# Spreading the conversion of layer 2's last five weight units over two steps each

## The chip, the cores and the metric

One core of a Trainium2 chip runs the whole program. The metric is the device time of one execution in microseconds (us), lower is better; the median of three runs stands below. The profile is of one execution of the same kernel.

## The reference, cut to what matters

```python
# 1: linear attention with decay, over 4 x 8 heads, 768 positions, head size 48
state = alpha[t][:, None] * state + outer(k[t], v[t]);  y[t] = q[t] @ state
# 2: x is the 3072 x 384 result. Tokens with x @ w_skip > 0 go through their best one of
#    8 experts (384 -> 1024 -> 384, relu), scaled by its softmax weight, and are added to x
# 3: layer 2, on all 3072 tokens
h = x @ w_in            # w_in  384 x 2048
g = h - tanh(h)
out = g @ w_out         # w_out 2048 x 384
```

The two matrices of layer 2 arrive in 64-bit floating point (they were scaled by a 64-bit number), all other inputs in 32-bit. The kernel reads the 64-bit words as pairs of 32-bit integers and converts them itself.

## The kernel before, in words

TensorE works on rounded 32-bit values (the type fp32r of the trace). To keep the precision, each operand is split in a high part (rounded) and a low part (the remainder), and each product is three matmuls: high by high, low by high, high by low.

**Stages.** Attention runs in 24 steps, with the routing of tokens to experts between them. The first units of layer 2 for its first 512 tokens follow, then the experts: a loop of `NMU + 4` = 68 steps, one for each 128 columns of an expert's hidden layer and four to drain. Then layer 2: its 2048 hidden columns are 16 weight units of 128 (`NF2`), its tokens six blocks of 512 (`nb`). The first block's units 0 to 4 (`NE0`) were done ahead of the experts, so layer 2's loop (`steps`, lines 871 to 897) has 91 steps: units 5 to 15 of block 0 are steps 0 to 10, block 1 begins at step 11.

**One step of layer 2.** `mm1b` (line 453) issues nine matmuls of 128x512 into a PSUM bank, line 464. Its `after` is a generator with four operations: tanh on ACT (L470), `g` = h minus tanh on DVE (L472), its high part `gh` on ACT (L474), its low part `gl` on DVE (L476). Then `mm2b` of the step two before issues twelve matmuls of 128x384 (L498). The banks of `mm1b` alternate between two, so the matmuls of step i wait for `g` of step i-2, which reads that bank last. The `g` line thus stands in the trace as what TensorE waits for.

**The weight units.** Units 0 to 4 were converted during attention and units 5 to 10 during the experts. The five late ones (`NLATE`), units 11 to 15, are converted in layer 2's own first ten steps; unit 11+k is first used by step 6+k. Each is loaded by one DMA of 768 KB into `raw64`, for which there is one buffer (`wload`, line 125), and converted by four functions (`wsplit`, lines 150 to 170), which the trace shows by line:

- `s0`: DVE `cs` (L155) and DVE `ca` (L156), both reading `raw64`; they repack the upper word.
- `s1`: ACT `cl` (L159), which reads the lower words of `raw64`, DVE `cs` again (L160, called cs2 here), ACT `wh` (L162), the high part, made from `ca`.
- `s2`: DVE `cl` times `cs` (L166, called cl2 here), DVE `ca` minus `wh` (L167, called ca2 here).
- `s3`: DVE `wl` (L170), the low part.

`cs`, `ca` and `cl` have one buffer each too.

**What sets the order.** Each engine works through its own queue in the order in which the program issues to it (`tc.manual_schedule()`); the lists `at[i]` and `aft[i]` say what is issued at the start and the end of step i. A transfer waits on SP's queue until its buffer's last reader is done. In the kernel before, late unit k has its load, `s0` and `s1` at the start of step 2k and `s2` and `s3` at the start of step 2k+1, all ahead of that step's matmuls, tanh, `g`, `gh` and `gl`. At the end of steps 3, 5, 7 and 9 `split2` transposes a quarter of the next block: three transposes on TensorE (L437), the high part `xh` on ACT (L439), the low part `xl` on DVE (L440). In the experts' loop, `result` of the last unit (L587, `xe`, two DVE operations that read the last expert's sums) is issued at step `NMU + 2`.

Of the kernel before, what the change touches and what calls it, by code (L numbers as in the profile page):

```python
# [33 lines left out]
NF, NF2 = FF // 128, FF2 // 128  # L34
# [3 lines left out]
NMU = NE * NF  # L38
# [5 lines left out]
NLATE = 5  # L44
# [17 lines left out]
def tile_kernel(ctx: ExitStack, tc: tile.TileContext, att0, att, vt, wsg, wmoe, wff, out):  # L62
# [56 lines left out]
    def wload(i):  # L119
        if i < NMU or not wide:  # L120
            raw_t[i] = rings["raw"].tile([128, W], F32, tag="raw", name=f"raw{i}")
            nc.sync.dma_start(raw_t[i], wmoe[i] if i < NMU else wff[i - NMU])
        else:
            raw_t[i] = cvp.tile([128, W, 2], U32, tag="raw64", name=f"raw{i}")
            nc.sync.dma_start(raw_t[i].rearrange("p a b -> p (a b)"), wff[i - NMU].bitcast(U32))

    def wsplit(i):

        own = (ring if i % RING < RING0 else rings["ring2"]) if i < NMU else ffE if i < NMU + NE0 else None
        late = i >= NMU + NF2 - NLATE  # L130
        t_ = {}

        def alloc():
            src = own or rings["late" if late else "R"]
            t_["h"] = src.tile([128, W], F32R, tag="wh", name=f"wh{i}")
            t_["l"] = src.tile([128, W], F32R, tag="wl", name=f"wl{i}")
            w_t[i] = (t_["h"], t_["l"])

        def n0():
            alloc()  # L140
            A.copy(t_["h"], raw_t[i])  # L141

        def n1():
            V.tensor_tensor(t_["l"], raw_t[i], t_["h"].bitcast(F32), ALU.subtract)  # L144

        if i < NMU or not wide:
            return [n0, n1]


        def s0():  # L150
            up = raw_t[i][:, :, 1]
            t_["s"] = cvp.tile([128, W], U32, tag="cs", name=f"cs{i}")
            t_["a"] = cvp.tile([128, W], U32, tag="ca", name=f"ca{i}")
            t_["f"] = cvp.tile([128, W], F32, tag="cl", name=f"cl{i}")
            V.tensor_scalar(t_["s"], up, 3, 0x3FFFFFFF, ALU.logical_shift_left, ALU.bitwise_and)  # L155
            V.scalar_tensor_tensor(t_["a"], up, 0xC0000000, t_["s"], ALU.bitwise_and, ALU.bitwise_or)  # L156

        def s1():
            A.activation(t_["f"], raw_t[i][:, :, 0], AF.Copy, scale=2.0 ** -52)  # L159
            V.tensor_scalar(t_["s"], t_["a"], 0xFF800000, None, ALU.bitwise_and)  # L160
            alloc()
            A.copy(t_["h"], t_["a"].bitcast(F32))  # L162

        def s2():
            a_ = t_["a"].bitcast(F32)
            V.tensor_tensor(t_["f"], t_["f"], t_["s"].bitcast(F32), ALU.mult)  # L166
            V.tensor_tensor(a_, a_, t_["h"].bitcast(F32), ALU.subtract)  # L167

        def s3():
            V.tensor_tensor(t_["l"], t_["a"].bitcast(F32), t_["f"], ALU.add)  # L170

        return [s0, s1, s2, s3]
# [252 lines left out]
    def rload(nb):  # L425
        d = X2[nb]
        d["r"] = rowp.tile([128, 4, RW], F32, tag="rows", name=f"rows{nb}")
        r0 = NS + 512 * nb
        i_ = nc.sync.dma_start(d["r"], xb[r0:r0 + 512, :].rearrange("(a p) d -> p a d", a=4))
        if 0 < nb < NIN // 512:  # L430
            tc.declare_no_dep(i_.ins, group="expert", reason="rows that no expert writes")
# [105 lines left out]
    def xload(e):  # L537
        E[e]["xe"] = rings["xe"].tile([128, 2, RW], F32, tag="xe", name=f"xe{e}")
        i_ = nc.sync.dma_start(E[e]["xe"], xb[e * CAP:(e + 1) * CAP, :].rearrange("(a p) d -> p a d", a=2))
        if e >= 2:  # L540
            tc.declare_no_dep(i_.ins, group="expert", reason="rows that no expert writes")
# [9 lines left out]
    def mm1(i):  # L551
        e, f = divmod(i, NF)
        d = E[e]
        wh, wl = w_t[i]
        hp = psY(f"hp{i}")[:, :CAP]
        n = 0
        for k in range(KT):
            ks = slice(128 * k, 128 * k + 128)
            for w_, x_ in ((wh, d["eh"]), (wl, d["eh"]), (wh, d["el"])):
                T.matmul(hp, w_[:, ks], x_[:, k], start=n == 0, stop=n == 3 * KT - 1)  # L560
                n += 1
        hh = rings["m2"].tile([128, CAP], F32R, tag="hh", name=f"hh{i}", bufs=3)
        hl = rings["m2"].tile([128, CAP], F32R, tag="hl", name=f"hl{i}", bufs=3)
        A.activation(hh, hp, AF.Relu)
        V.scalar_tensor_tensor(hl, hp, 0.0, hh.bitcast(F32), ALU.max, ALU.subtract)  # L565
        d[f] = (hh, hl)

    def mm2(i):
        e, f = divmod(i, NF)
        d = E[e]  # L570
        wh, wl = w_t.pop(i)
        hh, hl = d.pop(f)
        if f == 0:
            d["yp"] = [psB(f"yp{e}_{a}")[:, :DM] for a in range(2)]
        for a in range(2):
            o = d["yp"][a]
            sl_ = slice(128 * a, 128 * a + 128)
            T.matmul(o, hh[:, sl_], wh[:, DM:], start=f == 0, stop=False)  # L578
            T.matmul(o, hh[:, sl_], wl[:, DM:], start=False, stop=False)  # L579
            T.matmul(o, hl[:, sl_], wh[:, DM:], start=False, stop=f == NF - 1)  # L580
        if f < NF - 1:
            return
        xe = d["xe"]

        def result():
            for a in range(2):
                V.scalar_tensor_tensor(xe[:, a, :DM], d["yp"][a], xe[:, a, CGW:CGW + 1], xe[:, a, :DM],  # L587
                                       ALU.mult, ALU.add)

        def store():  # L590
            for a in range(2):
                s_ = nc.gpsimd.indirect_dma_start(
                    xb[:, :], bass.IndirectOffsetOnAxis(xe[:, a, CPOS:CPOS + 1].bitcast(U32), 0), xe[:, a, :], None,
                    bounds_check=TOP, oob_is_err=False)
                if e or a:
                    tc.declare_no_dep(s_.ins, group="expert", reason="rows of their own")
                tc.add_to_no_dep_group("expert", s_.ins)

        at[i + 3].append(result)
        at[i + 4].append(store)  # L600
# [81 lines left out]
    at, aft = collections.defaultdict(list), collections.defaultdict(list)  # L682
# [149 lines left out]
    at, aft = collections.defaultdict(list), collections.defaultdict(list)  # L832
# [18 lines left out]
    for e in range(1, NE):  # L851
        for a in range(2):
            aft[NF * e - 4 + a].append(lambda e=e, a=a: xprep(e, a))
        if e + 1 < NE:
            at[NF * e - 1].append(lambda e=e: xload(e + 1))
    at[20].append(lambda: rload(1))
    for i in range(NMU + 4):
        for f_ in at[i]:
            f_()
        if i < NMU:  # L860
            mm1(i)
        if 2 <= i < NMU + 2:
            mm2(i - 2)
        for f_ in aft[i]:
            f_()
# [3 lines left out]
    rings["x2", 1] = pool("p1", 1, ff_ctx, "right")  # L869
    rings["g"] = pool("g1", 2, ff_ctx, "right")  # L870
    steps = [(nb, f) for nb in range(NU // 4) for f in range(NF2) if nb or f >= NE0]
    at, aft = collections.defaultdict(list), collections.defaultdict(list)
    for k in range(NLATE):
        r = NMU + NF2 - NLATE + k
        at[max(0, 2 * k - 1 + 1)].append(lambda r=r: wload(r))
        for n, f_ in zip((0, 0, 1, 1), wsplit(r)):
            at[2 * k + n].append(f_)
    for nb in range(1, NU // 4):
        i = steps.index((nb, 0))
        for a in range(4):  # L880
# [4 lines left out]
    for i in range(len(steps) + 1):  # L885
        for f_ in at[i]:
            f_()
        if i < len(steps):
            issue, after = mm1b(*steps[i])
            issue()  # L890
            collections.deque(after(), 0)
        if 2 <= i < len(steps):
            mm2b(*steps[i - 2])
        elif i == len(steps):
            mm2b(steps[-1][0], *(f for _, f in steps[-2:]))
        for f_ in aft[i]:
            f_()
# [6 lines left out]
    with tc.If(past > 0):  # L904
# [17 lines left out]
        with tc.For_i(0, NC_, 1) as ci:  # L922
            with tc.For_i(0, B, 1) as bi:
# [23 lines left out]
                for f in range(NF2):  # L947
                    wh, wl = w_t[NMU + f]
                    hpd = psY(f"hp2d{f}")[:, :128]
                    n = 0  # L950
# [75 lines left out]
```

## Time and profile before

| what | value |
|---|---|
| time, median of 3 runs (lowest to highest) | 739.13 us (737.74 to 741.64) |
| the profiled execution: time, span | 738.44 us, 736.8 us |
| granted TensorE clock, mean | 0.986 |
| busy: PE, PE's weight load, DVE, ACT, POOL | 93%, 85%, 61%, 41%, 17% |
| L472 `g`, L476 `gl` (DVE, 96 each) | 66.3 us, 66.5 us |
| L470 tanh, L474 `gh` (ACT, 96 each) | 57.3 us, 59.5 us |
| L498 matmuls, three groups of 384 | 130.2, 130.4 and 129.9 us |
| L464 matmuls, three groups of 288 | 116.2, 114.2 and 114.3 us |

A busy share is a mean over the span; matmuls are pipelined, so one that is listed as 393 ns long lets the next start after about 230 ns. Layer 2's loop begins at 323.94 us of the span and the late units are converted until 372.5 us.

### The profile page before, as it was taken

How to read it: one execution, taken by the hardware profiler on the slowest of the kernel's cores; microseconds unless marked ns; L12 is line 12 of the kernel's file. 1: busy time of each engine (PE TensorE's matmuls, PEld its weight loads, DVE VectorE, ACT ScalarE, POOL GpSimd, SP SyncE). 2: the span in 40 equal slices, each digit the busy share in tenths (PEclk: the TensorE clock that was granted, in tenths of full speed). 3: DMA queues.
4: the chain of work that ended last, by engine and by line, in shares of the span. 5: the costliest groups of instructions: out<-in, count | busy, mean ns of one | idle time of the engine just before them, and what ended most of it. 6: DMA issues, size and time to landing. Idle time of an engine off the chain costs nothing.

```text
span 736.8 us, 11897 instructions
## 1 busy us (share of the span) xinstructions
PE 686.1 (93%) x4707; PEld 629.2 (85%) x4707; DVE 449.8 (61%) x736; ACT 301.7 (41%) x588; POOL 125.3 (17%) x121
## 2 busy tenths in 40 slices
PE   3999978899999999999979999999999999999993
PEld 2888867788999999997768999999899999889892
DVE  8999999966888888847744334333333333333331
ACT  2546544345666656624422233233323333333220
POOL 5433347441011111210002001000200020001002
PEclk9999999899999999999989999999999999999997
DMA  9899957346779778512111001001100110001001
GB/s 275 180 218 281 230 145 219 98 155 207 253 257 321 257 249 268 168 64 85 45 44 43 1 1 61 25 1 44 43 1 1 45 43 1 1 1 43 2 1 46
DMA packets 30542, 81.39 MB, mean 110 GB/s; under 512 B 4405, under 2 KB 14677, under 8 KB 30480
## 3 DMA queue, kind: packets, MB, share of 16 engines
q1 hardware_dynamic: 26384, 68.64, 32.3%
q0 software_dynamic: 4096, 11.92, 4.4%
q8 instruction: 39, 0.64, 0.4%
q14 instruction: 23, 0.19, 0.1%
HBM read 65.45 MB, written 15.84 MB: 110 GB/s over the span
## 4 chain that ended last, share of the span: by engine, by line
issue 55%; PE 26%; DVE 12%; POOL 3%; ACT 1%; DMA 1%; POOLq 0%; ACTq 0%; SPq 0%; DVEq 0%
PE hp L560 8%; PE yp L578 3%; PE yp L579 3%; PE yp L580 3%; DVE G L203 2%; POOL out_dram L512 2%; DVE F L196 2%; PE pa L229 2%; DVE am L234 2%; PE py L243 2%; PE px L296 1%; PE h L464 1%; PE py L250 1%; DVE kh L214 1%; POOL qh L209 1%
## 5 line engine op out<-in xcount | busy, mean ns | idle before, releaser
L472 DVE TENSOR_TENSOR g<-h,g 128x512 f32<-128x512 f32 x96 | 66.3, 691 | 162.8 <-ACT g L470 162.8
L498 PE MATMUL y<-wh,gh 128*128 128x384 f32 x384 | 130.2, 339 | 0.7 <-ACT gh L474 0.7
L498 PE MATMUL y<-wh,gl 128*128 128x384 f32 x384 | 130.4, 340 | 0.2
L498 PE MATMUL y<-wl,gh 128*128 128x384 f32 x384 | 129.9, 338 | 0.0
L470 ACT ACTIVATE g<-h 128x512 f32<-128x512 f32 x96 | 57.3, 598 | 168.1 <-PE h L464 168.1
L464 PE MATMUL h<-xh,wh 128*128 128x512 f32 x288 | 116.2, 403 | 3.2 <-DVE g L472 3.1
L464 PE MATMUL h<-xh,wl 128*128 128x512 f32 x288 | 114.2, 397 | 3.6 <-DVE wl L170 3.6
L464 PE MATMUL h<-xl,wh 128*128 128x512 f32 x288 | 114.3, 397 | 0.0
L476 DVE TENSOR_TENSOR gl<-g,gh 128x512 fp32r<-128x512 f32 x96 | 66.5, 693 | 65.9 <-ACT gh L474 44.0
L474 ACT CAST gh<-g 128x512 fp32r<-128x512 f32 x96 | 59.5, 620 | 91.4 <-DVE g L472 91.4
L512 POOL DMA_INDIRECT out_dram<-ob,id x24 | 23.6, 983 | 375.8 <-DVE ob L511 308.0
L498 PEld LDWEIGHTS y<-wh,gh 128*128 128x128 f32 x384 | 72.4, 189 | 5.2 <-ACT gh L474 1.3
L498 PEld LDWEIGHTS y<-wl,gh 128*128 128x128 f32 x384 | 72.5, 189 | 4.2
L498 PEld LDWEIGHTS y<-wh,gl 128*128 128x128 f32 x384 | 72.3, 188 | 1.6 <-DVE gl L476 1.6
L464 PEld LDWEIGHTS h<-xh,wh 128*128 128x128 f32 x288 | 54.4, 189 | 14.5 <-DVE g L472 5.8
L464 PEld LDWEIGHTS h<-xh,wl 128*128 128x128 f32 x288 | 54.6, 190 | 12.5 <-DVE wl L170 3.9
L464 PEld LDWEIGHTS h<-xl,wh 128*128 128x128 f32 x288 | 54.5, 189 | 12.5
L141 ACT CAST wh<-raw 128x768 fp32r<-128x768 f32 x64 | 53.5, 835 | 24.1 <-PE yp L580 22.3
L144 DVE TENSOR_TENSOR wl<-raw,wh 128x768 fp32r<-128x768 f32 x64 | 60.8, 950 | 2.8 <-ACT wh L141 2.8
L560 PE MATMUL hp<-eh,wh 128*128 128x256 f32 x192 | 55.7, 290 | 1.3 <-DVE hl L565 1.3
L229 PE MATMUL pa<-qh,kh 64*128 64x128 f32 x384 | 30.8, 303 | 27.9 <-POOL qh L209 19.5
L560 PE MATMUL hp<-eh,wl 128*128 128x256 f32 x192 | 53.8, 280 | 0.0
(140 smaller groups left out, 1164.5 us busy)
## 6 DMA issues: line engine op xcount, KB each, us to landing
raw<-in_wmoe_dram SPq DMA_DIRECT2D x64, 384.0 KB, 4.0
raw<-in_wff_dram SPq DMA_DIRECT2D x16, 768.0 KB, 5.3
it<-in_att_dram SPq DMA_DIRECT2D x40, 289.5 KB, 7.9
rows<-xb SPq DMA_DIRECT2D x6, 776.0 KB, 4.3
vt<-in_vt_dram SPq DMA_DIRECT2D x24, 192.0 KB, 5.6
xb<-zero SPq DMA_DIRECT2D x4, 776.0 KB, 7.3
xe<-xb SPq DMA_DIRECT2D x8, 388.0 KB, 4.9
it<-in_att_dram SPq DMA_DIRECT2D x2, 772.0 KB, 8.5
```

The lines of the kernel that those rows point to most:

```text
L141: A.copy(t_["h"], raw_t[i])
L144: V.tensor_tensor(t_["l"], raw_t[i], t_["h"].bitcast(F32), ALU.subtract)
L229: T.matmul(d["pa"][:, j, p], d["kh"][r, p], d["qh"][r, p], start=p == 0, stop=p == NP - 1)
L464: T.matmul(hp, *todo.pop(0), start=len(todo) == last, stop=not todo)
L470: A.activation(g, hp, AF.Tanh)
L472: V.tensor_tensor(g, hp, g, ALU.subtract)
L474: A.copy(gh, g)
L476: V.tensor_tensor(gl, g, gh.bitcast(F32), ALU.subtract)
L498: T.matmul(o, g_[:, sl_], w_[:, DM:], start=first and n == 0, stop=last and n == len(todo) - 1)
L512: s_ = nc.gpsimd.indirect_dma_start(out[:, :], bass.IndirectOffsetOnAxis(d["id"][:, a:a + 1], 0), ob, None, bounds_check=N - 1, oob_is_err ...
L560: T.matmul(hp, w_[:, ks], x_[:, k], start=n == 0, stop=n == 3 * KT - 1)
L578: T.matmul(o, hh[:, sl_], wh[:, DM:], start=f == 0, stop=False)
```

## The change: what it does

The four functions of each late unit move. A third list, `mid[i]`, holds what is issued inside step i's `after`, behind `gh` and ahead of `gl`.

- Late unit 0: its load is issued at step `NMU + 1` of the experts' loop and its `s0` at step `NMU + 3`; `s1` and `s2` at the start of layer 2's step 0, `s3` in the middle of step 0.
- Late unit k from 1 to 4: its load is issued at the start of step 0, 1, 3 or 5 (before: 2, 4, 6, 8), `s0` at the start of step 2k-1, `s1` in the middle of step 2k-1, `s2` at the start of step 2k, `s3` in the middle of step 2k.

No operation is added or left out, and no buffer is changed.

```diff
+    late = [wsplit(NMU + NF2 - NLATE + k) for k in range(NLATE)]
+    at[NMU + 1].append(lambda: wload(NMU + NF2 - NLATE))
+    at[NMU + 3].append(late[0][0])
     for i in range(NMU + 4):
...
-    at, aft = collections.defaultdict(list), collections.defaultdict(list)
+    at, mid, aft = (collections.defaultdict(list) for _ in range(3))
+
     for k in range(NLATE):
-        r = NMU + NF2 - NLATE + k
-        at[max(0, 2 * k - 1 + 1)].append(lambda r=r: wload(r))
-        for n, f_ in zip((0, 0, 1, 1), wsplit(r)):
-            at[2 * k + n].append(f_)
+        if k:
+            at[max(0, 2 * k - 3)].append(lambda k=k: wload(NMU + NF2 - NLATE + k))
+            at[2 * k - 1].append(late[k][0])
+        (mid[2 * k - 1] if k else at[0]).append(late[k][1])
+        at[2 * k].append(late[k][2])
+        mid[2 * k].append(late[k][3])
...
             issue, after = mm1b(*steps[i])
             issue()
-            collections.deque(after(), 0)
+            for n, _ in enumerate(after()):
+                if n == 2:
+                    for f_ in mid[i]:
+                        f_()
```

## Rows read from the trace of the kernel before

**Rows 1.** Stretches: busy us (instructions) of PE, PEld, DVE, ACT, POOL; PEclk, DMA, GB/s.

```profile
323.94:378.88 54.94, 48.16 (x220) 40.48 (x220) 40.67 (x59) 21.32 (x35) 2.25 (x2) 0.94 0.24 78
600.00:700.00 100.00, 100.00 (x508) 90.50 (x507) 36.03 (x55) 31.34 (x53) 3.89 (x4) 1.00 0.02 9
```

**Rows 2.** Timeline of PE, steps 0 to 12: start, us, line, [idle before, releaser].

```profile
323.94 0.40 PE L464 MATMUL h<-xh,wh 128*128 128x512 f32 x1
...
328.44 0.50 PE L464 MATMUL h<-xh,wh 128*128 128x512 f32 x1 [0.21 <-DVE g L472]
...
368.47 0.51 PE L464 MATMUL h<-xh,wh 128*128 128x512 f32 x1 [0.60 <-DVE g L472]
372.58 0.79 PE L464 MATMUL h<-xh,wl 128*128 128x512 f32 x1 [3.60 <-DVE wl L170]
...
378.88 0.39 PE L464 MATMUL h<-xh,wh 128*128 128x512 f32 x1
...
383.09 0.39 PE L464 MATMUL h<-xh,wh 128*128 128x512 f32 x1
```

**Rows 3.** Timeline of PE, transposes of a later block, with nothing to wait for.

```profile
416.61 0.49 PE L437 MATMUL px<-ident,rows 128*128 128x128 f32 x3
...
417.17 0.39 PE L464 MATMUL h<-xh,wl 128*128 128x512 f32 x1
```

**Rows 4.** Waits, 320 to 380 us: who for whom, us, times, longest.

```profile
PE h L464 <- DVE g L472: 3.1, 8, 0.7
```

**Rows 5.** Timeline of DVE: the first late unit, an `xl`, the last `wl`.

```profile
324.67 0.55 DVE L155 TENSOR_SCALAR cs<-raw 128x768 uint32<-128x768 uint32 x1
325.26 0.96 DVE L156 SCALAR_TENSOR_TENSOR ca<-raw,cs 128x768 uint32<-128x768 uint32 x1
326.25 0.56 DVE L160 TENSOR_SCALAR cs<-ca 128x768 uint32<-128x768 uint32 x1
327.69 0.69 DVE L472 TENSOR_TENSOR g<-h,g 128x512 f32<-128x512 f32 x1 [0.88 <-ACT g L470]
329.07 0.69 DVE L476 TENSOR_TENSOR gl<-g,gh 128x512 fp32r<-128x512 f32 x1 [0.69 <-ACT gh L474]
329.68 0.95 DVE L166 TENSOR_TENSOR cl<-cl,cs 128x768 f32<-128x768 f32 x1
330.55 0.95 DVE L167 TENSOR_TENSOR ca<-ca,wh 128x768 f32<-128x768 f32 x1
...
364.32 0.55 DVE L440 TENSOR_TENSOR xl<-px,xh 128x384 fp32r<-128x384 f32 x1
...
371.57 0.96 DVE L170 TENSOR_TENSOR wl<-ca,cl 128x768 fp32r<-128x768 f32 x1
```

**Rows 6.** Timeline of ACT in the same stretch.

```profile
326.33 0.84 ACT L162 CAST wh<-ca 128x768 fp32r<-128x768 f32 x1 [4.19 <-DVE ca L156]
...
333.13 0.62 ACT L474 CAST gh<-g 128x512 fp32r<-128x512 f32 x1 [3.59 <-DVE g L472]
333.65 0.91 ACT L159 ACTIVATE cl<-raw 128x768 f32<-128x768 uint32 x1
...
363.58 0.47 ACT L439 CAST xh<-px 128x384 fp32r<-128x384 f32 x1
```

**Rows 7.** SP's own waits; the load issued at 326.30; landing of `raw`, 300 to 370 us.

```profile
SPq L125 <- DVE ca L156: 43.4, 4, 22.5
...
raw<-in_wff_dram SPq DMA_DIRECT2D x1, 768.0 KB, 4.7
...
DMA to landing us min/median/max: 3.0/4.2/5.3
```

**Rows 8.** Timeline of PE in attention: the matmuls behind an idle time.

```profile
109.50 1.16 PE L229 MATMUL pa<-qh,kh 64*128 64x128 f32 x16 [2.69 <-POOL qh L209]
```

**Rows 9.** Stretches, columns as in Rows 1: behind that idle time; in step 10.

```profile
109.50:113.00 3.50, 3.50 (x37) 3.28 (x37) 3.36 (x5) 1.68 (x5) 3.04 (x3) 1.00 1.00 301
373.00:375.00 2.00, 2.00 (x6) 1.52 (x6) 1.28 (x3) 1.00 (x2) 0.00 (x0) 0.50 0.00 0
```

## The prediction

> **What bounds the kernel now.** I read the busy shares by stretch first, then the waits of the stretch that the change touches, then the timelines of TensorE, DVE and ACT beside each other. From step 11 to the end of the matmuls TensorE is the bound: the row for 600 to 700 us shows it busy for all of the 100 us at a granted clock of 1.00 [rows 1]. So whatever moves the start of step 11 moves the end by as much, and only the ten steps of the late units are open. There TensorE is busy 48.2 of 54.9 us, and DVE 40.7 us, twice its share later on [rows 1].
>
> What those steps should cost comes from undisturbed ones. Step 11 to step 12 is 383.09 - 378.88 = 4.21 us [rows 2]. Three transposes and the matmul behind them take 417.17 - 416.61 = 0.56 us [rows 3], and a matmul at full clock follows the one before after 0.23 us, so a quarter of `split2` adds 0.33 us. Steps 2 to 10 hold nine steps and four quarters: 9 x 4.21 + 4 x 0.33 = 39.2 us. They took 378.88 - 328.44 = 50.4 us [rows 2], so 11.2 us are lost, in three parts. (a) In step 10 the second matmul waits for `wl` of the last unit: 372.58 instead of 368.47 + 0.23, so 3.9 us [rows 2]. (b) The clock then stands at 0.50, the lower of its two levels, 1.2 GHz [rows 9]: from 372.58 to 378.88 are 6.3 us [rows 2], where the remaining 20 matmuls of a step take 4.21 - 0.23 = 3.98, so 2.3 us. (c) The other 5.0 us are eight waits for `g` of 0.2 to 0.7 us, 3.1 us in TensorE's own rows [rows 4], with the slower first matmul behind each (0.50 for 0.39 us [rows 2]).
>
> Why `g` is late: DVE is a queue that has become longer than TensorE's step. A unit's `wl` comes about 10.0 us after the one before (the first follows its ca2 of 330.55 at about 331.5, the last starts at 371.57, four units later [rows 5]), where TensorE needs 2 x 4.21 + 0.33 = 8.75 us for two steps. In these 10 us DVE stands still twice for `gh` (0.69 us each) and once for tanh (0.88 us), which sits on ACT behind `wh`, which waits for `ca` [rows 5, 6]. The loads are not the limit: SP waits for `ca` to release `raw64`, and a load lands 5.3 us later at most [rows 7], in half of the 10 us.
>
> **The change part by part.** Nothing is added or dropped: a load and eight operations of each of five units change places. Times below are on the clock of the trace of before; in a queue an operation starts 0.08 us before its predecessor's listed end if it doesn't need its result (0.87 for 0.95 us, 329.68 to 330.55) and 0.03 us behind it if it does [rows 5].
>
> *First unit.* Its load was issued at SP ahead of everything in layer 2 already (its row is not among SP's four waits for `ca` [rows 7]), so its new place gives nothing. Its `s0` is issued at step `NMU + 3`, but `result`, two operations that wait for the experts' last matmul, at `NMU + 2`. DVE's order is still `xe`, `cs`, `ca`, and `cs` stays at 324.67: no gain. What changes is that cl2 and ca2 now stand ahead of `g` of step 0 instead of behind it. `wh` runs until 327.17 [rows 6], so it doesn't delay ca2: cs2 at 326.25, cl2 at 326.84, ca2 at 327.71, `g` at 328.58 instead of 327.69. Step 2 starts at 329.3 instead of 328.4: a loss of 0.9 us.
>
> *Units 1 to 4.* DVE's order for two steps becomes `cs`, `ca`, `g`, cs2, `gl`, (`xl`), cl2, ca2, `g`, `wl`, `gl`. cs2 (0.56) and `wl` (0.95) now fill the 0.69 us in which DVE waited for `gh`, and the tanh no longer waits for `wh`. What takes over is a chain through ACT: `cl` and `wh` stand behind `gh` and ahead of `xh`, and `xl` waits for `xh`. From `cs`: `cs` 0.59, `ca` 0.87, `g` 0.72, `gh` 0.53, `cl` 0.82, `wh` 0.75, `xh` 0.51, `xl` 0.47, cl2 0.87, ca2 0.87, `g` 0.61, `wl` 0.87, `gl` 0.61, together 9.1 us, from the durations of [rows 5, 6] less overlap. That is 0.9 less than before, but 0.35 more than TensorE's 8.75: DVE still falls behind, slowly.
>
> *The load as a new wait.* `raw64` is now released by `cl`, and the next `cs` moved forward by a step. `cl` ends 0.59 + 0.87 + 0.72 + 0.53 + 0.91 = 3.62 us behind its `cs`, the transfer is issued 0.1 us later and lands 4.2 us after that (median; 3.0 to 5.3 [rows 7]): 7.9 us from `cs` to `cs`, hidden under the chain of 9.1. Queued behind a `cs` that waits are `ca`, `g`, cs2 and `gl`. This cover of 1.2 us is the thin place of the change. It isn't there for units 1 and 2: load 1 is issued at 326.30 and lands after 4.7 us [rows 7], so `cs` of unit 1 starts at 331.05, where DVE is free at 330.7; step 1 has no `xh`, so `cs` of unit 2 comes 7.9 us later, at 338.95. Then 9.1 us each: 348.05 and 357.15. The last `wl` is 7.6 us behind its `cs` (9.1 less `wl` and `gl`): 364.75, ending at 365.7 instead of 372.5.
>
> *TensorE.* From 329.3 it needs 8 x 4.21 + 4 x 0.33 = 35.0 us to step 10: 364.3. On the way `g` of step 6 ends at 348.05 + 7.0 + 0.69 = 355.75, where step 8 is due at 329.3 + 6 x 4.21 + 3 x 0.33 = 355.55: 0.2 us. Step 10 starts at 364.5, its second matmul is due at 364.75 and waits for `wl` until 365.75: 1.0 us. The remaining 20 matmuls take 3.98 + 0.1. Step 11 starts at 369.8 instead of 378.9, so the gain is 9.1 us, if the clock stays up. That it does I take from an idle time of 2.69 us in attention, behind which the granted clock is 1.00 [rows 8, 9]; only behind the 3.60 us does it fall here. I take 9.0 us: 738.44 - 9.0 = 729.4 for the profiled execution, whose span is 736.8, and from the median, 0.7 above it, 730.1.
>
> The bounds of the sum: with no stall left at all the gain is 11.2 us (727.9). With every landing at 5.3 us, `cs` of unit 1 is 0.6 later and `cs` of unit 2 another 1.1; 9.0 us per round then still hides under 9.1, so the gain is 9.0 - 1.7 = 7.3 (731.8); if that longer stall in step 10 also drops the clock, 5.0 (734.1).
>
> **The rivals.** *The clock falls on short stalls.* The stall of 1.2 us ahead of step 2 (0.9 more than before) and that of 1.0 in step 10 each cost up to the 2.3 us of part (b): a gain of 6.7 with one, 4.4 with both (732.4 to 734.7). Against it: eight short waits and one of 2.69 us left it at 1.00; the mean of 0.94 over the stretch [rows 1] is filled by step 10 alone, 6.5 us at half of full speed being 3.3 of 54.9 us. In the Trainium skill, the page "TensorE: Matmul & The Clock Gate", section "A second HAM failure mode: psum-queue depth-cycling", says that TensorE's frequent small idle times between groups of matmuls over alternating PSUM banks can make its clock go up and down; by that rule this rival holds. The trace so far disagrees with it: it shows such idle times in steps 2 to 9 with the clock up.
>
> *The load takes the place of the wait.* With a landing L beyond 5.4 us each round is 3.7 + L. `cs` of unit 4 is at 326.3 + L + 3 x (3.7 + L); the gain is gone when its `wl` ends as late as now, at 372.5, so `cs` at 364.0 and L = 6.6 us: 739. For it: a single buffer and DVE held by the wait. Against it: nothing else moves data here, and the longest landing was 5.3 [rows 7].
>
> *Slower: `raw64` is released late.* The program issues load k (k of 2 and more) at the start of step 2k-3, ahead of `s1` of unit k-1 in the same step, which still reads the old contents. If the release is not counted from that reader but from the unit's end in step 2k-2 (`wl`), the round becomes `wl`'s end, 8.55 us behind `cs`, + 0.1 + 4.2 = 12.9 us with DVE standing still for some 4 us each time. From 331.05 `cs` of unit 4 is then at 369.7 and its `wl` ends at 378.3, 5.8 us later than now, with the same drop of the clock: 745. It decides against the change once the release comes 2.4 us behind `cl`, by the L above. For it: only the order in the text; against it: on SP's queue today the wait is for the last reader, `ca` [rows 7], not for the unit's end.
>
> **How the numbers follow.** The forecast (gain 7.3 to 11.2) has 0.74, the clock's rival 0.10, the load's 0.08 (near no change), the slower one 0.08. About 0.5%, 3.7 us, is what can be told from no change here. The first two are faster by more: 0.84; same 0.08; slower 0.08. The range takes in the full gain and the clock's rival: 727.5 to 734.7.
>
> **What would show it.** Right: `cs` at 324.67 still behind `xe`; step 2 near 329.3; cs2 and `wl` directly behind `g`; `xl` waiting for `xh` some 1.3 us; `cs` of units 3 and 4 waiting for no DMA; step 10 waiting 0.5 to 1.5 us for `wl` with the clock at 1.00; step 11 near 369.8; equal times from there. Wrong: `cs` waiting for `raw` in each round, a granted clock of 0.50 in steps 2 or 10, or a last `wl` beyond 368.

## The result, and the profile after

The changed kernel takes 729.11 us (median of four runs, 727.78 to 729.88) against 739.27 us (737.74 to 741.64): a ratio of 0.987, interval 0.9847 to 0.9893. In a second measurement, six runs against twelve of the kernel before, the ratio was 0.9877 (0.9852 to 0.9901). 730.1 had been forecast, a ratio of 0.9877 to the 739.13 us known then.

The page's head shows the same busy time as before within 3.2 us on every engine, in a span that is 10.1 us shorter; the dip of PEclk in slice 21 is gone. One in slice 8 is gone too: it lies in attention, which the change doesn't touch, and comes and goes in the other profiles.

```profile
span 726.7 us, 11899 instructions
...
PE 682.9 (94%) x4707; PEld 628.1 (86%) x4707; DVE 448.0 (62%) x736; ACT 301.4 (41%) x588; POOL 125.1 (17%) x121
...
PEclk9999999999999999999999999999999999999997
```

The stretch from step 0 to step 11, in the columns of [rows 1], is 45.72 us long instead of 54.94, at a granted clock of 1.00 instead of 0.94:

```profile
323.68:369.40 45.72, 44.17 (x221) 38.75 (x220) 39.06 (x58) 20.71 (x35) 2.26 (x2) 1.00 0.29 93
```

TensorE's timeline after, answering to [rows 2]; these two waits are the only ones left to it in the stretch:

```profile
323.68 0.40 PE L464 MATMUL h<-xh,wh 128*128 128x512 f32 x1
...
329.15 0.50 PE L464 MATMUL h<-xh,wh 128*128 128x512 f32 x1 [1.18 <-DVE g L472]
...
364.45 0.49 PE L464 MATMUL h<-xh,wh 128*128 128x512 f32 x1
365.32 0.50 PE L464 MATMUL h<-xh,wl 128*128 128x512 f32 x1 [0.37 <-DVE wl L170]
...
369.40 0.39 PE L464 MATMUL h<-xh,wh 128*128 128x512 f32 x1
```

DVE's timeline after, answering to [rows 5]: the first unit, `cs` of all five, an `xl`, the last `wl`.

```profile
324.42 0.55 DVE L155 TENSOR_SCALAR cs<-raw 128x768 uint32<-128x768 uint32 x1
...
328.41 0.68 DVE L472 TENSOR_TENSOR g<-h,g 128x512 f32<-128x512 f32 x1
329.01 0.95 DVE L170 TENSOR_TENSOR wl<-ca,cl 128x768 fp32r<-128x768 f32 x1
...
330.79 0.56 DVE L155 TENSOR_SCALAR cs<-raw 128x768 uint32<-128x768 uint32 x1 [0.23 <-DMA raw<-in_wff_dram]
...
338.72 0.56 DVE L155 TENSOR_SCALAR cs<-raw 128x768 uint32<-128x768 uint32 x1 [0.38 <-DMA raw<-in_wff_dram]
...
347.75 0.56 DVE L155 TENSOR_SCALAR cs<-raw 128x768 uint32<-128x768 uint32 x1
...
352.49 0.56 DVE L440 TENSOR_TENSOR xl<-px,xh 128x384 fp32r<-128x384 f32 x1 [1.22 <-ACT xh L439]
...
356.77 0.55 DVE L155 TENSOR_SCALAR cs<-raw 128x768 uint32<-128x768 uint32 x1
...
364.32 0.94 DVE L170 TENSOR_TENSOR wl<-ca,cl 128x768 fp32r<-128x768 f32 x1
```

SP's own waits in the stretch (who for whom, total, times, longest), answering to [rows 7]. The last row is new: three of the four loads now wait for `cl`.

```profile
SPq L125 <- DVE ca L156: 32.6, 4, 22.5
...
SPq L125 <- ACT cl L159: 6.1, 3, 2.0
```

Where the 10.1 us of span are: 0.26 before step 0 (323.94 and 323.68), 9.22 between step 0 and step 11, none from there to the last output transfer (step 11 and that transfer's issue both moved by 9.48 us), and 0.6 behind it, where the programs only end. So the change is worth 9.2 us in this profile and the rest lies outside it. The second ratio, 0.9877 or 9.1 us, agrees, but its interval is wide (7.3 to 11.0 us), so that it meets the forecast to the fourth digit is chance.

### The profile page after: what moved, and what is told of

It reads as the page before. It is cut to its first block, busy times and chain, and to the rows that moved or that the text cites. A ratio compares the mean times of both kernels' runs of the same rounds, so it can differ in the third digit from the quotient of the medians.

```text
span 726.7 us, 11899 instructions
## 1 busy us (share of the span) xinstructions
PE 682.9 (94%) x4707; PEld 628.1 (86%) x4707; DVE 448.0 (62%) x736; ACT 301.4 (41%) x588; POOL 125.1 (17%) x121
## 4 chain that ended last, share of the span: by engine, by line
issue 54%; PE 25%; DVE 13%; POOL 3%; DMA 2%; ACT 1%; SPq 0%; POOLq 0%; DVEq 0%
PE hp L560 8%; PE yp L578 3%; PE yp L580 3%; PE yp L579 3%; DVE G L203 3%; DVE F L196 2%; POOL out_dram L512 2%; DVE am L234 2%; DMA it<-in_att_dram 2%; PE h L464 1%; PE py L243 1%; PE pa L229 1%; PE y L498 1%; DVE kh L214 1%; PE px L296 1%
```

## The experiments

The common yardstick is the start of a step's first matmul, counted from step 0 of the same profile. This table is read off TensorE's timelines; "time" is the ratio to the kernel before with its interval where there were several rounds, or one run and, behind it, one of the kernel before on the same chip.

| kernel | step 2 | step 10 | step 11 | time |
|---|---|---|---|---|
| before | 4.50 | 44.53 | 54.94 | 1 |
| changed | 5.47 | 40.77 | 45.72 | 0.987 |
| again | 5.46 | 40.47 | 45.39 | 0.9877 (0.9852 to 0.9901) |
| e1_spread | 4.13 | 38.90 | 44.28 | 0.9865 (0.9843 to 0.9887) |
| e2_advance | 6.45 | 46.50 | 50.81 | 0.9944 (0.9922 to 0.9966) |
| e8_both | 4.13 | 39.02 | 43.23 | 0.9849 (0.9825 to 0.9873) |
| e3_load_at_use | 5.46 | 40.48 | 45.40 | 732.99; 737.94 |
| e4_release_late | 5.46 | 55.18 | 60.08 | 747.17; 737.94 |
| e6_xh_first | 5.46 | 40.49 | 44.70 | 732.79; 737.94 |
| e7_unit0_first | 4.13 | 38.90 | 43.54 | 730.50; 737.94 |
| e5_load_twice | 5.47 | 54.98 | 59.93 | 740.64; 737.20 |
| e9_wl_x3 | 5.46 | 40.35 | 47.20 | 728.20; 737.20 |
| e9_wl_x5 | 5.46 | 40.72 | 51.87 | 736.09; 737.20 |

Step 0 itself lies between 321.7 and 331.3 us in these profiles, so single times differ by up to 10 us for what happens ahead of layer 2; the steps are what the verdicts rest on. Three profiles with the same order of work on the engines (changed, again, e3_load_at_use) have step 11 at 45.72, 45.39 and 45.40, so a difference of 0.3 us between two profiles says nothing.

**The changed kernel again.** No edit.

> The changed kernel once more, as the yardstick for the others: 729.1 us as in its first four runs, 45.7 us from the start of step 0 to the start of step 11 (54.9 before). If the 0.9 us by which the first measurement beat the sum were chance outside the changed stretch, the ratio to before moves towards 0.9877 (a gain of 9.1).

The ratio came out at 0.9877 and step 11 at 45.39 us. The first profile puts what the first measurement had over the sum outside the stretch; the two ratios, whose intervals overlap almost wholly, don't decide it.

**Spread alone (e1_spread).**

```diff
-    at[NMU + 1].append(lambda: wload(NMU + NF2 - NLATE))
-    at[NMU + 3].append(late[0][0])
...
-        if k:
-            at[max(0, 2 * k - 3)].append(lambda k=k: wload(NMU + NF2 - NLATE + k))
-            at[2 * k - 1].append(late[k][0])
-        (mid[2 * k - 1] if k else at[0]).append(late[k][1])
-        at[2 * k].append(late[k][2])
-        mid[2 * k].append(late[k][3])
+        at[max(0, 2 * k - 2)].append(lambda k=k: wload(NMU + NF2 - NLATE + k))
+        at[2 * k].append(late[k][0])
+        mid[2 * k].append(late[k][1])
+        at[2 * k + 1].append(late[k][2])
+        mid[2 * k + 1].append(late[k][3])
```

The load of unit k from 1 to 4 also stands two steps earlier in the program than in the kernel before; e3_load_at_use, below, shows what such a place is worth in the changed kernel.

> Spread alone: each late unit keeps the steps it had before the change (unit k in steps 2k and 2k+1), but s1 and s3 stand in the middle, between gh and gl. Theory (DVE's queue had become longer than TensorE's step, and filling its waits shortens it): the rounds of DVE shrink below TensorE's 8.75 us for two steps, since without xh behind wh in the same step the xl doesn't wait; g of step 0 isn't delayed, so step 2 starts 4.2 us behind step 0 instead of 5.5; the last wl comes about 39.9 us behind step 0, so step 10 waits 1.5 us at full clock; step 11 is 44.9 us behind step 0, 0.8 less than in the changed kernel: 728.3 us. Rival (the gain came from the units being begun a step earlier): the last unit is again ready only in step 9's end, step 10 waits 3.9 us and the clock falls, 54.9 - about 5 us of small waits at best: step 11 at 49.9 or later, 734 us or more.

Step 11 at 44.28, less than the theory's 44.9, and far from the rival's 49.9. DVE's timeline: `cs` to `cs` is 7.9 us and no `xl` waits, since `cl` and `wh` stand in the even steps and `xh` in the odd ones.

```profile
346.17 0.55 DVE L155 TENSOR_SCALAR cs<-raw 128x768 uint32<-128x768 uint32 x1
...
349.01 0.69 DVE L476 TENSOR_TENSOR gl<-g,gh 128x512 fp32r<-128x512 f32 x1 [0.22 <-ACT gh L474]
...
353.63 0.55 DVE L440 TENSOR_TENSOR xl<-px,xh 128x384 fp32r<-128x384 f32 x1
354.10 0.55 DVE L155 TENSOR_SCALAR cs<-raw 128x768 uint32<-128x768 uint32 x1
...
362.03 0.55 DVE L155 TENSOR_SCALAR cs<-raw 128x768 uint32<-128x768 uint32 x1
```

A round is 2.2 us shorter than the 10.1 us of before. The waits for `gh` gave 1.2 of them (0.69 us twice before, 0.22 once now), and the wait for tanh 0.8 (0.80 us before, none now, since `wh` no longer stands ahead of it on ACT). The last `wl` is still late, and step 10 waits for it, though less than the 1.5 us forecast:

```profile
369.01 0.50 PE L464 MATMUL h<-xh,wl 128*128 128x512 f32 x1 [0.81 <-DVE wl L170]
```

So the spreading alone gives 10.7 us of the stretch, more than the whole change; the two times, 0.9865 and 0.9877, can't be told apart.

**Advance alone (e2_advance).**

```diff
         if k:
-            at[max(0, 2 * k - 3)].append(lambda k=k: wload(NMU + NF2 - NLATE + k))
+            at[2 * k - 1].append(lambda k=k: wload(NMU + NF2 - NLATE + k))
             at[2 * k - 1].append(late[k][0])
-        (mid[2 * k - 1] if k else at[0]).append(late[k][1])
-        at[2 * k].append(late[k][2])
-        mid[2 * k].append(late[k][3])
+        at[max(0, 2 * k - 1)].append(late[k][1])
+        at[2 * k].append(late[k][2])
+        at[2 * k].append(late[k][3])
```

> Advance alone: units 1 to 4 start a step earlier as in the change, the first unit ahead of the layer too, but all operations of a step stand at its start again, none between gh and gl. Theory: DVE's rounds stay at about 10.1 us; the last wl is ready 4.2 us earlier, in time, so the waits of 3.9 us and the half clock in step 10 are gone, but nine waits for g of 0.5 to 0.7 us stay and step 2 starts 2 us later than before; step 11 is 50.9 us behind step 0, a gain of 4.0: 735.2 us. Rival (the advance is the whole gain): 45.7 us and 729 us.

Step 11 at 50.81 (50.9 forecast), a ratio of 0.9944 where 735.2 us had been given (0.9945). The last `wl` is in time, and DVE's rounds stay at 10.1 us:

```profile
353.39 0.96 DVE L170 TENSOR_TENSOR wl<-ca,cl 128x768 fp32r<-128x768 f32 x1
...
363.50 0.96 DVE L170 TENSOR_TENSOR wl<-ca,cl 128x768 fp32r<-128x768 f32 x1
...
373.61 0.96 DVE L170 TENSOR_TENSOR wl<-ca,cl 128x768 fp32r<-128x768 f32 x1
```

One thing was not as expected: behind the wait of 2.16 us ahead of step 2 the clock fell. The first row is of TensorE's timeline, the second of the stretch behind it, in the columns of [rows 1].

```profile
335.18 0.50 PE L464 MATMUL h<-xh,wh 128*128 128x512 f32 x1 [2.16 <-DVE g L472]
...
335.23:337.73 2.50, 2.50 (x8) 1.98 (x9) 1.88 (x3) 1.38 (x2) 0.00 (x0) 0.68 0.02 6
```

Step 2 took longer for it (5.86 us to the start of step 3, not 4.21), and the waits for `g` are six, of 0.4 to 2.2 us, instead of nine. As DVE's rounds set the pace here, the slower matmuls fell into waits that would have come anyway. That the sum still fits is what a bound by DVE predicts; the expectation's count of waits was wrong.

**Both remaining stalls taken away (e8_both), and each alone (e7_unit0_first, e6_xh_first).** The first edit; for the second, `split2` of block 1 is cut in its three parts, the transposes issued behind `issue()` and `xh` put first in `mid`.

```diff
-    at[NMU + 3].append(late[0][0])
+    at[NMU + 2].append(late[0][0])
...
+            if nb == 1:
+                turn_, high, low = split2_parts(nb, a)
+                post[i - 8 + 2 * a].append(turn_)
+                mid[i - 8 + 2 * a].insert(0, high)
+                aft[i - 8 + 2 * a].append(low)
...
+            for f_ in post[i]:
+                f_()
```

> The changed kernel with both remaining stalls taken away: s0 of the first unit is issued ahead of result (DVE stands still there for 1.8 us), and in steps 3, 5, 7 and 9 the transposes follow the step's first nine matmuls and xh stands ahead of cl and wh on ACT, so that xl doesn't wait. Theory (two chains, through the first unit's place and through ACT's order, set what is left): no wait for g at step 2, none for wl at step 10, step 11 is 43.3 us behind step 0, 2.4 less than in the changed kernel: 726.7 us. Rival (the load is the thin place): cl comes 0.4 us later and cs waits for raw 0.3 to 0.5 us in each round, which the theory absorbs; if the load were the limit, the last wl would come no earlier and step 11 stay at 45.7 us.

> The changed kernel with one edit: s0 of the first late unit is issued one step earlier, ahead of result, in DVE's idle time of 1.8 us. Theory: the wait of 1.2 us ahead of step 2 goes, all later units come 1.5 to 1.8 us earlier, step 10 waits for wl 0.6 us at most; step 11 is 44.0 us behind step 0. Rival (only the last wl's time counts and the stall of step 2 is given back by step 10): 45.4 us.

> The changed kernel with one edit: in steps 3, 5, 7 and 9 the transposes follow the step's first nine matmuls, and xh stands ahead of cl and wh on ACT. Theory: xl no longer waits 1.1 to 1.2 us in three rounds, cs waits for raw about 0.5 us in rounds 3 and 4 instead, DVE's round falls from 9.0 to 8.4 us, step 10 waits for nothing; step 2's wait of 1.2 us stays. Step 11 is 44.6 to 44.9 us behind step 0. Rival (the load holds the round): 45.4 us or more.

With both, step 11 is at 43.23 (43.3 forecast), and TensorE is busy for the whole stretch. From step 2 to step 11 are 39.10 us, where the prediction's sum of undisturbed steps gave 39.2: nothing of the loss is left.

```profile
331.33:374.56 43.23, 43.23 (x220) 38.77 (x220) 37.77 (x56) 21.07 (x35) 2.32 (x2) 1.00 0.28 99
```

`cs` waits for `raw` twice, 0.4 us in all, as the theory allowed. The ratio of 0.9849 overlaps that of the changed kernel in its interval; the medians, 731.28 and 733.51 us on the same chip, differ by as much as the step 11 times do (2.2 us). It is the fastest of the kernels by the stretch; by time alone, with these rounds, it can't be told from the changed one.

The first unit's place alone gives 43.54 (44.0 forecast): DVE's `cs` and `ca` now run ahead of `xe` and the wait of step 2 is gone.

```profile
325.86 0.55 DVE L155 TENSOR_SCALAR cs<-raw 128x768 uint32<-128x768 uint32 x1
326.44 0.96 DVE L156 SCALAR_TENSOR_TENSOR ca<-raw,cs 128x768 uint32<-128x768 uint32 x1
327.75 1.14 DVE L587 SCALAR_TENSOR_TENSOR xe<-yp,xe 128x384 f32<-128x384 f32 x2 [0.34 <-PE yp L580]
```

The last `wl` is still 0.4 us late for step 10.

ACT's order alone gives 44.70 (44.6 to 44.9 forecast): step 10 no longer waits, step 2's wait of 1.17 us stays, and `cs` waits for its load twice, 0.9 us in all. Both rivals fall: step 2's stall isn't given back, and the load doesn't hold the rounds.

**Loads issued late (e3_load_at_use).**

```diff
-            at[max(0, 2 * k - 3)].append(lambda k=k: wload(NMU + NF2 - NLATE + k))
+            at[2 * k - 1].append(lambda k=k: wload(NMU + NF2 - NLATE + k))
```

> The changed kernel, but each load of units 1 to 4 is issued directly ahead of its s0 in step 2k-1, one or two steps later in the program than in the change. Theory (SP has nothing else to do, so a load starts when cl of the unit before releases raw64, wherever it is issued): nothing moves, step 11 is 45.4 to 45.7 us behind step 0, cs waits for raw 0.2 and 0.4 us for units 1 and 2 and not for 3 and 4. Rival (the earlier loads are part of the gain): cs waits for up to 4 us in each round, step 11 at 55 us or later.

45.40 against 45.39 in the changed kernel again: the place of the loads in the program is worth nothing here. `cs` waited for `raw` once, 0.3 us.

**The slower rival made real (e4_release_late).**

```diff
             V.tensor_tensor(t_["l"], t_["a"].bitcast(F32), t_["f"], ALU.add)
+            if late:
+                scr = cvp.tile([128, 1], U32, tag="scr", name=f"scr{i}")
+                V.tensor_copy(scr, raw_t[i][:, 0:1, 0])
```

> The changed kernel with one more reader of raw64: a copy of one column (128x1) on DVE behind each late unit's wl, so that the buffer is released at the unit's end. This is the slower rival of the prediction, made real. Theory: cs waits for raw 3.6 to 4.2 us in each of four rounds, DVE's round becomes 13 us, g is late for steps 3, 5, 7 and 9 by 2.3 to 3.4 us, and step 11 is 60.8 us behind step 0 with the clock up, up to 68 if three of these waits also drop it: slower than before (54.9) by 6 us or more. Rival (DVE has room that the prediction didn't see): 45.7 to 54.9 us.

60.08 us, slower than before by 5.1 us in the stretch (747.17 against 737.94 us, single runs). DVE's waits in the stretch, total, times, longest:

```profile
DVE cs L155 <- DMA raw<-in_wff_dram: 14.6, 4, 3.8
```

The price that the prediction gave to this rival, 5.8 us over before, was near in size, but it is not paid where the prediction put it. There the last `wl` was late and the clock fell behind the wait in step 10. Here the last `wl` does end 7.4 us later behind step 0 than before, but step 10 waits for it by only 0.36 us and keeps its clock; TensorE has lost the time earlier, in waits for `g` (2.81 and 3.11 us ahead of steps 3 and 7, as the expectation had them, but only 0.82 and 1.13 ahead of 5 and 9), and the clock fell behind the two long ones. The expectation's 60.8 us was meant for a clock that stays up. What this rival hung on, whose reading releases the buffer, went the good way in the changed kernel, as SP's waits for `cl` above show.

**The landing doubled (e5_load_twice).**

```diff
-            nc.sync.dma_start(raw_t[i].rearrange("p a b -> p (a b)"), wff[i - NMU].bitcast(U32))
+            for _ in range(2 if i >= NMU + NF2 - NLATE else 1):
+                nc.sync.dma_start(raw_t[i].rearrange("p a b -> p (a b)"), wff[i - NMU].bitcast(U32))
```

> The changed kernel with each late unit's load done twice, one transfer after the other into the same buffer, so that the landing doubles from about 4.2 to about 8.4 us. The prediction put the point where the gain is gone at a landing of 6.6 us. Theory: a round becomes 3.7 + 8.4 = 12.1 us, cs waits for raw 2.8 to 4.2 us in each of four rounds, g is late for steps 3, 5, 7 and 9, and step 11 is 59 us behind step 0 with the clock up and up to 66 us if it falls behind the longest waits (before: 54.9). Rival (loads have more cover than the chain on paper gives): under 50 us.

59.93 us where 59 was forecast for a landing of 8.4 with the clock up (a transfer landed 4.1 to 4.3 us after its issue). `cs` waited for its load in each of the four rounds, by 2.8 to 4.4 us. The clock did fall, behind waits of 3.43 and 1.97 us, and as in e2_advance and e4_release_late the sum without it still comes near: DVE's rounds set the end. The single one's 4.1 to 4.7 us leave the change room, as the sum had it, and a transfer of twice the length takes more than the whole gain.

**The clock behind a wait (e9_wl_x3, e9_wl_x5).**

```diff
-            V.tensor_tensor(t_["l"], t_["a"].bitcast(F32), t_["f"], ALU.add)
+            for _ in range(3 if i == NMU + NF2 - 1 else 1):   # 5 in e9_wl_x5
+                V.tensor_tensor(t_["l"], t_["a"].bitcast(F32), t_["f"], ALU.add)
```

> The changed kernel with wl of the last late unit computed three times over (two more DVE operations of 0.87 us each, same result), so that step 10 waits about 2.1 us instead of 0.4. Theory (idle times up to 2.7 us left the clock at 1.00 in attention): the wait grows by 1.75 us and the granted clock stays at 1.00 behind it: step 11 at 47.2 us. Rival (short waits cost the clock): 1.2 GHz behind the wait, 49.5 us.

> The same with wl of the last unit computed five times over: step 10 waits about 3.9 us, as in the kernel before. Theory (part b of the loss belongs to a wait of this length): the clock falls to 0.50 behind it and 2.3 us are lost on top of 3.5: step 11 at 51.2 us. If the clock stays up here too, the fall in the kernel before had another cause: 48.9 us.

The wait of 2.29 us left the clock at 1.00 and step 11 came at 47.20 (47.2 forecast):

```profile
365.09 0.49 PE L465 MATMUL h<-xh,wl 128*128 128x512 f32 x1 [2.29 <-DVE wl L171]
...
369.16 0.39 PE L465 MATMUL h<-xh,wh 128*128 128x512 f32 x1
...
365.16:366.96 1.80, 1.80 (x8) 1.50 (x9) 1.11 (x3) 0.69 (x2) 0.00 (x0) 1.00 0.65 242
```

Behind 4.33 us it was 0.50 and step 11 came at 51.87 (51.2 forecast). Step 10 itself began 0.37 us later here, so the two are compared from the delayed matmul to the start of step 11, 20 matmuls in both: 4.07 us with the clock up (365.09 to 369.16), 6.31 with the clock down (369.87 to 376.18). So 2.2 us are the clock's, near the 2.3 of part (b). Both waits are longer than forecast because a repeated `wl` took 0.99 us and not 0.87.

```profile
369.87 0.80 PE L465 MATMUL h<-xh,wl 128*128 128x512 f32 x1 [4.33 <-DVE wl L171]
...
376.18 0.40 PE L465 MATMUL h<-xh,wh 128*128 128x512 f32 x1
...
369.91:371.91 2.00, 2.00 (x5) 1.61 (x6) 1.32 (x3) 0.86 (x2) 0.00 (x0) 0.50 0.00 0
```

## Why the prediction was right

*What moves the end.* Step 11 and the last output transfer moved by the same 9.48 us: right.

*What was lost.* The sum of undisturbed steps, 39.2 us, holds: e8_both runs them in 39.10. For part (c), 5.0 us, the rows that the prediction shows cover only 4.0: 3.1 of waits and eight slower first matmuls of 0.11 each. TensorE's weight loads in the same stretch show a ninth wait and more idle time:

```profile
PEld h L464 <- DVE g L472: 5.8, 9, 0.9
```

*The first unit.* `cs` is still behind `xe`, and step 2 started 5.47 us behind step 0 instead of 4.50: a loss of 0.97 where 0.9 was said. e7_unit0_first shows that this loss was the place of one function, and that all later units hang on it: undoing it brings 1.9 us (43.54 against 45.39 in again).

*The rounds.* 9.1 us were forecast; from 338.72 to 347.75 and 356.77 they are 9.03 and 9.02. `xl` waits for `xh` up to 1.22 us (1.3 said), and `cs` of units 1 and 2 waits for its load by 0.23 and 0.38 us, of units 3 and 4 not at all. e6_xh_first confirms the chain through ACT.

*Step 10.* The last `wl` starts 40.64 us behind step 0 (40.8 said); the second matmul starts 0.87 us behind the first instead of 0.23, so 0.6 us of wait for the forecast 1.0. Step 10 itself began 0.2 us later than said (40.77 for 40.56). These two small misses go against each other, and step 11 is at 45.72, where 45.9 was said; the 0.2 us of waiting forecast for step 8 don't show as a wait.

*The clock.* It stayed at 1.00, so part (b) came back in full. The rule of the Trainium skill that stood for the clock's rival (page "TensorE: Matmul & The Clock Gate", section "A second HAM failure mode: psum-queue depth-cycling") does not show in this stretch: neither the changed kernel's wait of 1.18 us nor the eight short ones of before pulled the clock down. My ground for a clock that stays up was weaker than it looked. I leaned on one idle time of 2.69 us with the clock up; in e2_advance it fell behind 2.16 us. The waits that came, 1.18 and 0.6 us, were short enough for the conclusion to hold; the reason was not general.

*What the gain is made of.* The prediction did not say which half of the change earns it. e1_spread and e2_advance do: spreading alone takes 10.7 us out of the stretch, advancing alone 4.1, both together 9.2 to 9.6. The earlier start isn't useless once the units are spread: e8_both, which has it without its costs, is 1.05 us ahead of e1_spread (43.23 and 44.28). But in the changed kernel it costs 2.2 us (45.39 in again against 43.23), at step 2 and in ACT's order (`cl` and `wh` ahead of `xh` in the same odd step), so on balance it takes back 1.1 us, or 1.4 by the first profile. These are single profiles; the times don't tell these kernels apart.

## What to carry to other kernels

Before asking which operation is late, add up the queue of the engine that issues it over one round, with its waits in it, and compare that with the round of the engine that should be the bound: here 10.0 against 8.75 us, and each wait that TensorE showed followed from it. Filling a queue's own waits with work that is due anyway shortens the round; moving the same work earlier only moves the date, and may put it ahead of something that was in time. Where a single buffer is loaded, moving its first reader forward spends the cover of the load, so work out from the last reader to the next first one whether the landing still fits.

## What the runs showed of the hardware

The length of one idle time of TensorE between about 2.0 and 2.8 us does not say whether the granted clock falls. It stayed at 1.00 behind 2.29 us (e9_wl_x3) and 2.69 us [rows 8, 9], and fell behind 2.16 us (e2_advance, shown above), behind 1.97 us in e5_load_twice (the first two rows), and behind 2.81 us in e4_release_late (the last two):

```profile
359.00 0.50 PE L465 MATMUL h<-xh,wh 128*128 128x512 f32 x1 [1.97 <-DVE g L473]
...
359.03:361.03 2.00, 2.00 (x7) 1.57 (x8) 1.07 (x2) 2.00 (x3) 0.00 (x0) 0.72 0.05 12
...
340.83 0.79 PE L467 MATMUL h<-xh,wh 128*128 128x512 f32 x1 [2.81 <-DVE g L475]
...
340.84:342.84 2.00, 2.00 (x5) 1.61 (x6) 1.66 (x3) 2.00 (x3) 0.00 (x0) 0.50 0.00 0
```

Waits up to 1.69 us never cost it in these steps, and the four of 3.11 us and more (3.11, 3.43, 3.60 and 4.33) all did. What decides in between, these runs don't settle.
